# Second MoE matmul of an attention + MoE kernel: seven block products per granule pair in place of eight

## The chip, the cores and the metric

The kernel runs on one core of a Trainium2 chip. The metric is the device time in microseconds (us) of one execution. Executions of the kernel before agree within 0.4%. A run more than 1.5% above the fastest of the same kernel is labelled slow and left out of the ratios. The profile is of one execution; its span (first to last instruction) is about 2 us shorter than the measured time. Each experiment ran in the same rounds and on the same chip as the kernel before, whose medians lie between 217.01 and 217.14 us in the five batches; two experiments are compared with each other only through it.

Engines: TensorE (PE in the profile, its weight loads PEld), VectorE (DVE), ScalarE (ACT), GpSimd (POOL); SP is the queue that issues most DMAs (79 of 155 in the trace before, 74 from GpSimd's).

## The reference

```python
# q, k, v: [4, 8, 768, 64]; 8 global keys, 96 local keys
scores = q @ k.T / 8 + bias(distance, head)        # masked outside global or local keys
x = (softmax(scores) @ v) -> [3072, 512]           # heads side by side
h = x @ w_in                                       # [3072, 2048]
g = s * relu(h) ** 2 + b
out = g @ w_out                                    # [3072, 512], float32
```

The two last lines are computed as `s * (relu(h)**2 @ w_out) + b * colsum(w_out)`, so the second MoE matmul takes the squares in bf16, and its evacuation from PSUM multiplies by `s` and adds the constant row `bvec`.

## The kernel before: the parts that matter

The 3072 tokens are cut into 12 granules of 256 tokens. Attention of granule j takes two *steps*, 2j and 2j+1, each of two head pairs. The MoE work of earlier granules is put between the pieces of attention, so that TensorE always has something to do. In the traces VectorE and TensorE run their instructions in the order of the program (VectorE's timeline below, 107.57 to 115.01 us, and PE's, 143.85 to 155.97 us, are two such stretches).

```python
def p1_mm(j, fp):                 # two 128-row blocks of h for granule j
    ps = ps_h.tile([P, 2, GT], F32, tag="psh")            # 3 PSUM buffers "psh" in all
    for i in range(2):
        for kc in range(KC):      # 4: 8 matmuls of 256 columns in all
            nc.tensor.matmul(ps[:, i, :], lhsT=w_in_bf[...], rhs=xT[j][:, kc, :], ...)
    def relu():   nc.scalar.activation(gs, ps[:], ACT.Relu)             # ScalarE
    def square(): nc.vector.tensor_tensor(gs, gs, gs, ALU.mult)         # VectorE, 512 wide

def p2_mm(j, tb):                 # second matmul: 128 tokens, 16 matmuls of 512 columns
    po = ps_h.tile([P, DM], F32, tag="psh")
    for fc in range(FC):
        nc.tensor.matmul(po[:], lhsT=gT[j][:, fc, tb*P:(tb+1)*P], rhs=w_out_bf[:, fc, :], ...)

def p2_out(j, tb):                # VectorE evacuates: s * po + bvec, then DMA out
    nc.vector.scalar_tensor_tensor(out=o_sb[:], in0=po, scalar=s_bc[:], in1=bvec[:],
                                   op0=ALU.mult, op1=ALU.add)

def stage_A(u):                   # attention-value product of one head pair
    av = ps_av.tile(...)          # the ONLY attention buffer in PSUM
    ... matmuls pt x (v or voff) ...
    normalize(xn, av)             # VectorE: reciprocal and product; only then is av free

def step(s, c0, c1, c2):
    run(scores(s + 1))            # scores, exp (ScalarE), mask (VectorE) of the next step
    if first step of the granule: make_voff(j)            # VectorE copies the shifted values
    run(c0);  stage_A(2 * s);     flush()                 # flush: output evacuations
    if first step: make_koff(j + 1)
    run(c1);  stage_A(2 * s + 1); run(c2)
    if last step of the granule: finish_granule(j)        # DMA-transposes xn[j] into xT[j]

# the steady schedule: in each step one p2 (128 tokens) and four p1 pieces (...)
for j in range(7, NJ):
    step(2*j,     p2[j-3][1:2], p1[j-2][4:6], p1[j-2][6:8])
    step(2*j + 1, p2[j-2][0:1], p1[j-1][0:2], p1[j-1][2:4])
```

The softmax here doesn't subtract the row's maximum and nothing guards it: scores larger than these inputs give would overflow.

## Time and profile before

| | before |
|---|---|
| median time | 217.11 us (216.98 to 217.18, 4 runs) |
| span of the profile | 215.4 us |
| PE busy, idle (span less busy) | 209.8, 5.6 us |
| DVE busy | 140.5 us |
| mean granted TensorE clock | 0.999 |

The page's first part gives busy time by engine, the second the busy tenths of each fortieth of the span; PEclk is the granted TensorE clock in tenths (9 is 90% or more).

```profile
PE 209.8 (97%) x2013; PEld 143.8 (67%) x2013; DVE 140.5 (65%) x344; ACT 113.6 (53%) x175; POOL 67.0 (31%) x89
...
PE   6999999999999999999999999999999999999993
...
PEclk9999999999999999999999999999999999999999
```

TensorE is busy in every slice. From the chain of waits (start in us, length, engine, tile and line, number of instructions), one step:

```profile
136.73 0.44 PE ps_s L395 x12
137.18 3.56 PE ps L611 x16
140.74 0.18 PE ps_av L446 x6
140.92 1.75 PE ps L566 x16
142.66 0.18 PE ps_av L446 x6
142.84 1.75 PE ps L566 x16
```

Each piece starts where the last one ends, so TensorE alone sets the pace: a step is 3.5 us of second matmul (16 of 512 columns, 216 ns from start to start), twice 1.75 us of first matmul (16 of 256 columns, 109 ns each) and the small attention products. The waits view of PE, which lists what it waited for, holds one line for everything after 85 us (the columns: total us, times, longest):

```profile
PE ps_av L446 <- DVE xn L420: 0.2, 1, 0.2
```

The groups that give the costs (busy, mean ns of one, then idle before them and its releaser):

```profile
L579 DVE TENSOR_TENSOR gT<-gT 128x512 bf16<-128x512 bf16 x96 | 40.4, 424 | 24.2 <-ACT gT L576 22.2
...
L411 DVE TENSOR_TENSOR pt<-pt,tmpl 128x1024 bf16<-128x1024 bf16 (+1 forms) x40 | 25.6, 650 | 9.3 <-ACT pt L404 8.6
...
L622 DVE SCALAR_TENSOR_TENSOR o_sb<-ps,s_bc,bvec 128x512 f32<-128x512 f32 x19 | 14.1, 744 | 9.9 <-PE ps L611 9.9
```

A bf16 product on VectorE costs 0.424 us for 512 elements and, in the 1024-wide form of the second line alone, 0.693 us; an evacuation of 512 costs 0.744 us. VectorE is idle for a third of the time, and that idle time is what the change means to use.

### The profile page before, as it was taken

The numbers are of one execution on the slowest core, as the hardware profiler recorded it, in microseconds if no ns is written. First come the engines' busy times: TensorE is split into PE (matmuls) and PEld (weight loads), VectorE is DVE, ScalarE is ACT, GpSimd is POOL, SyncE is SP. The second block draws the span as 40 slices with busy tenths as digits, with TensorE's granted clock in tenths as the row PEclk, the third lists the DMA queues.
The fourth block names the chain that finished last, engine by engine and source line by source line (L and its number), as shares of the span: only waits on it lengthen the run. The fifth ranks groups of instructions, "written<-read, shape, count | busy, mean of one in ns | idle before, by whom it ended". The sixth has DMA issues, their size and how long they took to land.

```text
span 215.4 us, 4939 instructions
## 1 busy us (share of the span) xinstructions
PE 209.8 (97%) x2013; PEld 143.8 (67%) x2013; DVE 140.5 (65%) x344; ACT 113.6 (53%) x175; POOL 67.0 (31%) x89
## 2 busy tenths in 40 slices
PE   6999999999999999999999999999999999999993
PEld 2578885557866575776676676676676676665852
DVE  3497579995989668985675675666676663432421
ACT  4675668585975564554644643544644642240610
POOL 8873335897646104506318045000000000000000
PEclk9999999999999999999999999999999999999999
DMA  5999999999999997999999949952310310311102
GB/s 166 197 177 206 207 206 173 152 152 127 117 150 138 157 183 110 156 255 171 208 133 171 171 79 159 132 102 72 97 50 5 97 52 24 73 52 49 49 3 97
DMA packets 107079, 27.33 MB, mean 127 GB/s; under 512 B 97712, under 2 KB 104112, under 8 KB 107056
## 3 DMA queue, kind: packets, MB, share of 16 engines
q0 software_dynamic: 72864, 12.85, 82.2%
q1 hardware_dynamic: 33136, 13.64, 34.5%
q10 hardware_dynamic: 1056, 0.52, 0.9%
q8 instruction: 16, 0.26, 0.5%
q14 instruction: 7, 0.06, 0.1%
HBM read 27.26 MB, written 6.29 MB: 156 GB/s over the span
## 4 chain that ended last, share of the span: by engine, by line
PE 91%; DVE 5%; DMA 2%; issue 0%
PE ps L566 38%; PE ps L611 35%; PE ps_s L395 5%; PE ps_av L446 5%; DMA first<-in_k_dram 2%; PE ps_2c L668 2%; DVE pt L411 1%; PE ps_t L269 1%; PE ps_s L372 1%; PE ps_w L155 1%; PE ps_s L468 1%; PE ps_x L542 1%; PE ps_t L301 1%; DVE o_early L644 1%; DVE wsum L589 1%; DVE xn L420 1%
## 5 line engine op out<-in xcount | busy, mean ns | idle before, releaser
L576 ACT ACTIVATE gT<-ps 128x512 bf16<-128x512 f32 x96 | 57.0, 598 | 76.4 <-PE ps L566 76.4
L566 PE MATMUL ps<-xT,w_in_bf 128*128 128x256 bf16 x768 | 90.2, 273 | 0.0
L611 PE MATMUL ps<-w_out_bf,gT 128*128 128x512 bf16 x368 | 83.9, 380 | 0.0
L566 PEld LDWEIGHTS <-w_in_bf 128*128 128x128 bf16 x768 | 72.7, 98 | 8.9
L611 PEld LDWEIGHTS <-gT 128*128 128x128 bf16 x368 | 34.4, 98 | 39.2
L579 DVE TENSOR_TENSOR gT<-gT 128x512 bf16<-128x512 bf16 x96 | 40.4, 424 | 24.2 <-ACT gT L576 22.2
L404 ACT ACTIVATE pt<-ps_s 128x1024 bf16<-128x1024 f32 (+1 forms) x44 | 39.2, 948 | 6.4 <-PE ps_s L395 6.4
L411 DVE TENSOR_TENSOR pt<-pt,tmpl 128x1024 bf16<-128x1024 bf16 (+1 forms) x40 | 25.6, 650 | 9.3 <-ACT pt L404 8.6
L104 POOL DMA_DIRECT2D nat<-in_k_dram x22 | 19.7, 895 | 8.1 <-DMA w_in_bf<-in_moe_w_in_dram 3.0
L104 POOL DMA_DIRECT2D nat<-in_q_dram x22 | 19.6, 891 | 8.3 <-DMA w_out_bf<-in_moe_w_out_dram 3.4
L105 POOL DMA_DIRECT2D vb<-in_v_dram x22 | 19.8, 900 | 5.7 <-DMA w_out_bf<-in_moe_w_out_dram 2.1
L420 DVE TENSOR_TENSOR xn<-ps_av,rc 128x256 bf16<-128x256 f32 x48 | 20.4, 425 | 1.7
L622 DVE SCALAR_TENSOR_TENSOR o_sb<-ps,s_bc,bvec 128x512 f32<-128x512 f32 x19 | 14.1, 744 | 9.9 <-PE ps L611 9.9
L446 PEld LDWEIGHTS <-pt 128*128 128x128 bf16 x320 | 14.6, 97 | 5.9 <-DVE xn L420 0.8
L419 DVE RECIPROCAL rc<-ps_av 128x4 f32<-128x4 f32 x48 | 8.5, 178 | 14.8 <-PE ps_av L446 13.5
L446 PE MATMUL ps_av<-vb,pt 128*128 128x65 bf16 x208 | 15.4, 193 | 0.4 <-DVE xn L420 0.2
L110 POOL COPY gate<-xT 1x1 bf16<-1x1 bf16 x6 | 1.2, 202 | 40.6 <-DMA xT<-xn 37.9
L446 PE MATMUL ps_av<-voff,pt 128*128 128x65 bf16 x112 | 10.5, 193 | 0.0
L395 PE MATMUL ps_s<-qk 64*128 64x128 bf16 x208 | 10.0, 224 | 0.0
L589 DVE TENSOR_TENSOR wsum<-wsum,w_out_bf 128x512 f32<-128x512 f32 x14 | 9.6, 686 | 0.2
L395 PEld LDWEIGHTS <-qk 64*128 64x128 bf16 x208 | 6.2, 96 | 5.3 <-issue 3.2
L155 PE MATMUL ps_w<-idle 128*128 128x256 bf16 (+1 forms) x19 | 5.2, 434 | 1.2 <-DVE idle L145 1.2
(77 smaller groups left out, 107.6 us busy)
## 6 DMA issues: line engine op xcount, KB each, us to landing
out_dram<-o_sb SPq DMA_DIRECT2D x19, 256.0 KB, 3.5
nat<-in_k_dram POOLq DMA_DIRECT2D x22, 128.0 KB, 7.5
nat<-in_q_dram POOLq DMA_DIRECT2D x22, 128.0 KB, 7.4
vb<-in_v_dram POOLq DMA_DIRECT2D x22, 128.0 KB, 7.5
w_in_bf<-in_moe_w_in_dram POOLq DMA_DIRECT2D x4, 512.0 KB, 11.6
w_out_bf<-in_moe_w_out_dram POOLq DMA_DIRECT2D x4, 512.0 KB, 17.9
out_dram<-o_early SPq DMA_DIRECT2D x4, 256.0 KB, 6.6
first<-in_q_dram ACTq DMA_DIRECT2D x2, 256.0 KB, 4.9
```

What stands on the lines that cost most here:

```text
L104: nc.gpsimd.dma_start(t[:, n, i, :, :], rows_of(srcs[n], b, sb))
L105: nc.gpsimd.dma_start(vbuf[b % 2][:, sb, :, 0:D], rows_of(v, b, sb))
L395: nc.tensor.matmul(ps[:, hi, oc * P : (oc + 1) * P], lhsT=kt[rows], rhs=qt[rows], start=not bias, stop=not bias or part * GB + n == len(pl ...
L404: nc.scalar.activation(pt[:, :, 0:ncol], ps[:, :, 0:ncol], ACT.Exp, scale=QSCALE)
L411: nc.vector.tensor_tensor(pv, pv, m.rearrange("p h a c -> p h (a c)"), ALU.mult)
L420: nc.vector.tensor_tensor(dst, av[:, :, :, 0:D], rc[:].to_broadcast((P, 2, 2, D)), ALU.mult)
L446: nc.tensor.matmul(av[:, i, hi, 0 : D + 1], lhsT=pt[:, hi, c * P : (c + 1) * P], rhs=vv, start=(n == 0), stop=(n == len(terms) - 1),)
L566: nc.tensor.matmul(ps[:, i, :], lhsT=w_in_bf[:, kc, fc * P : (fc + 1) * P], rhs=xT[j][:, kc, :], start=(kc == 0), stop=(kc == KC - 1),)
L576: nc.scalar.activation(gs, ps[:], ACT.Relu)
L579: nc.vector.tensor_tensor(gs, gs, gs, ALU.mult)
L611: nc.tensor.matmul(po[:], lhsT=gT[j][:, fc, tb * P : (tb + 1) * P], rhs=w_out_bf[:, fc, :], start=(fc == 0), stop=(fc == FC - 1),)
L622: nc.vector.scalar_tensor_tensor(out=o_sb[:], in0=po_cur.pop((j, tb))[:], scalar=s_bc[:], in1=bvec[:], op0=ALU.mult, op1=ALU.add,)
```

## The change

For granules 4 to 11 two granules A and B (256 tokens each) and the two halves of the 2048 inner rows make a 2 x 2 block matrix; so do the halves of the inner rows and of the 512 output columns of `w_out`. The Strassen-Winograd form needs seven block products instead of eight, with sums of blocks before and after. TensorE's second matmul falls by an eighth; VectorE gets the sums.

```diff
+    weight_sums: t1 = w12 - w11;  t2 = w22 - t1;  t3 = w22 - w12 (into w12);  t4 = w21 - t2     # 2048 wide, once
+    def g_sums(j, q):                      # j is the odd granule; q a quarter of its first matmul; 1024 wide
+        if q < 2:  s3 = A1 - B1
+        else:      s1 = B1 + B2;  s2 = s1 - A1;  s4 = A2 - s2
+    def unit_p1(j, q):                     # four blocks of h at a time
+        for fp in (2*q, 2*q + 1): p1_mm; relu
+        nc.vector.tensor_tensor(gs, gs, gs, ALU.mult)          # one square, 1024 wide
+        if j % 2: g_sums(j, q)
+    def product(pr, n):                    # 2 x 8 matmuls of 256 columns into one "psh" buffer
+        1: A1 w11   2: A2 w21   3: s4 w22   4: B2 t4   5: s1 t1   6: s2 t2   7: s3 t3
+    def evac(pr, n):                       # VectorE, from PSUM
+        1: r = s*P1 + bias (twice)   6: r += s*P6 (both, 1024 wide)   5: r1 += s*P5
+        2: store r0 + s*P2           7: store r1 + s*P7; r0 += s*P7
+        3: store r1 + s*P3           4: store r0 + s*P4
@@ step @@
         stage_A(2 * s + 1, pool)
+        flush()
@@ schedule (u1(j, q) is unit_p1, pe(pair, n) a product and its evacuation) @@
-    step(13, p2[4][0:1], p1[5][0:2], p1[5][2:4])
-    for j in range(7, NJ):
-        step(2 * j, p2[j - 3][1:2], p1[j - 2][4:6], p1[j - 2][6:8])
-        step(2 * j + 1, p2[j - 2][0:1], p1[j - 1][0:2], p1[j - 1][2:4])
+    step(12, [rest(3, 1)], [u1(4, 2)], [u1(4, 3)] + weight_sums[1:2])
+    step(13, [u1(5, 0), u1(5, 1)], [u1(5, 2)], [u1(5, 3)] + weight_sums[2:4] + spread)
+    step(14, [pe(2, 1), pe(2, 2)], [pe(2, 6), pe(2, 5)], [u1(6, 0)])
+    for j in (7, 9, 11):                   # pr = (j - 3) // 2
+        if j > 7: step(2 * j, [pe(pr, 2), pe(pr, 6)], [pe(pr, 5)], [u1(j - 1, 0)])
+        step(2 * j + 1, [pe(pr, 7), pe(pr, 3)], [pe(pr, 4)], [u1(j - 1, 1)])
+        step(2 * j + 2, [u1(j - 1, 2), u1(j - 1, 3)], [pe(pr + 1, 1)], [u1(j, 0)])
+        step(2 * j + 3, [u1(j, 1), u1(j, 2)], [u1(j, 3)], [])            # "odd step": all late sums
```

(Abbreviated; tiles that were needed only early share memory with the new ones. The last pair runs after the attention, with products in the order 1, 2, 7, 5, 6, 4, 3.)

## The prediction

> **What bounds the kernel now.** TensorE. The page gives PE 97% busy of a 215.4 us span, DVE 65%, ACT 53%. The waits view for PE from 105 us to the end is empty, and the chain of waits is 91% PE, running from 89 us on as an unbroken series of matmul groups. A two-head-pair step lasts 8.08 us, of which second matmul 3.45, first matmul 3.5, scores 0.55, attention-value about 0.5.
>
> **What the change removes.** In the chain a 256-column matmul costs 109 ns (32 in 3.49 us) and a 512-column one 216 ns (16 in 3.45 us)[...]. So splitting columns is nearly free and seven for eight is real: per granule pair 64 x 216 = 13.8 us becomes 112 x 109 = 12.2 us. Four pairs: about 6.7 us off PE, all critical. That is the whole possible gain (3.1%).
>
> **What it adds, on VectorE.** Durations read: bf16 product 512 wide 0.424, 1024 wide 0.693, output evacuation 512 wide 0.743; instructions without a dependency follow about 0.08 closer than these. 2048 wide then is about 1.2 (estimate from the slope), the PSUM evacuation 1024 wide 1.2-1.3 (estimate). [...] Per pair: eight sums +5.2; evacuations 7.0 in place of 3.0; wide squares -1.6. Once: four weight sums +4.9. Total +35 us: DVE about 175 us busy.
>
> **How much is on the critical path.** From the granule-4 stage to the end of attention (about 88-184 us) a pair's four steps hold about 30.6 us of PE work and 29 us of DVE work even at the closer spacing. The average nearly fits; its distribution doesn't. The step finishing an odd granule has 6.35 us of PE work but about 9.1 us of DVE work (two masks, squares, all sums). Its second attention-value product needs the only attention PSUM buffer, whose normalize stands in the in-order DVE queue behind the sums. Walking the steps by hand with the durations above:
> - that step: PE waits about 2.3 us for normalize; twice.
> - the following steps: about 1.4 us per pair for PSUM buffers whose evacuations come late, and for the transposed attention output, whose source is normalized late (landing now 3.2 us); twice.
> - first pair: the last two weight sums follow the sums at the end of step 13; the fourth product (5) then waits about 4 us for the evacuation of product 1; other waits 2.5 us.
> - tail: the last evacuations queue on DVE, about 1.2 us.
> Sum about +14 to 15 us of PE waits against -6.7; some may overlap better than I walked, so I take +13.
>
> **Prediction: 223.5 us, 217 to 228 in 8 of 10.** Faster by over 2%: 0.09; within 2%: 0.28; slower by over 2%: 0.63.
>
> **Right if** PE busy falls below about 93%, matmul count rises by about 190, second-product matmuls stay near 109 ns each in unbroken runs; DVE busy is near 175 us; the chain of waits shows much more DVE (normalize, sums, evacuations); PE or its weight loads idle before attention-value matmuls on normalize, before products and first matmuls on PSUM evacuations; one gap of several us in the first products.
>
> **Wrong if** 1024-wide sums on strided halves are much cheaper or dearer than 0.69; DVE spacing is closer so that lag never reaches the single attention buffer (then about 211-214); PE really runs slower for these products (weight loads 98 ns against 109 leave little slack), or its clock drops after the long gap (then above 228).

The two estimates of VectorE follow from the trace before. The product grows by 0.269 us from 512 to 1024 wide (0.424 to 0.693), so 2048 wide comes to 1.23; the changed kernel's weight sums took 1.21 to 1.22. Evacuations of 128, 384 and 512 took 0.352, 0.618 and 0.744 us (L676 and L622), so 1024 comes to 1.28; those of the changed kernel took 1.275 to 1.285 (L775). The closer spacing of 0.08 us is there too: the copy after the 0.74 us evacuation from 141.51 starts at 142.17.

## The result and the profile after

The changed kernel took 231.80 us (231.25 to 234.41, 4 runs) against 217.11. Ratios here are the mean time of one kernel's fast runs over the mean of the other's in the same rounds, so they are not quite the ratios of the medians: 1.07 (95% interval 1.0645 to 1.0756), so 7% slower. The prediction said 223.5, within 217 to 228: the direction was right, the size was not.

The page of the changed kernel:

```profile
PE 210.0 (92%) x2189; PEld 163.6 (71%) x2189; DVE 175.8 (77%) x364; ACT 114.2 (50%) x178; POOL 68.8 (30%) x89
...
PE   6999999999999999998298999699999699999981
...
PEclk9999999999999999999979999979999979999998
```

TensorE's busy time is the same as before although it does an eighth less of the second matmul in granules 4 to 11, PE now shows slices of 2 and 6 inside, and PEclk dips to 7 in three slices. Spans and clocks:

| | before | after | difference |
|---|---|---|---|
| span | 215.4 | 229.5 | +14.1 |
| PE idle (span less PE busy) | 5.6 | 19.5 | +13.9 |
| PE busy | 209.8 | 210.0 | +0.2 |
| DVE busy | 140.5 | 175.8 | +35.3 |
| mean granted clock | 0.999 | 0.973 | |

Run 8 below, with the same arithmetic and the full clock up to its last matmul, has 204.3 us of PE busy time. So the +0.2 is two things: about -5.5 us of matmul work saved and about +5.7 us of slower matmuls. (The clock record, read alone, gives 5.1 us for the latter: three stretches of 3.41 us at half clock. A fourth begins after the last matmul; it lowers the mean clock and costs nothing.)

PE's waits from the same point on:

```profile
PE ps_av L447 <- DVE xn L421: 5.3, 4, 2.2
PE ps_av L447 <- DVE voff L354: 4.3, 1, 4.3
PE ps_last L766 <- DVE o_last L775: 1.9, 1, 1.9
```

Part of the same waits is listed with the weight loads, which now come first in a wait. The chain of waits in an odd step (step 17), where before it was TensorE alone:

```profile
143.81 0.61 ACT gT L581
...
144.44 0.70 DVE gT L741
...
145.16 0.70 DVE gsum L731
...
145.89 0.70 DVE gsum L732
...
146.61 0.69 DVE gsum L733
...
147.43 0.44 DVE xn L421
...
148.77 5.27 PE ps L766 x32
```

ScalarE's relu releases the square (gT), then come three sums (gsum), and only then the normalize (xn) that frees the one attention buffer for TensorE. The last line holds the second effect, slow matmuls: 32 of 256 columns took 5.27 us where 32 take 3.5. The timeline of PE shows the same place (last bracket: idle before, and releaser):

```profile
143.85 1.91 PE L571 MATMUL ps<-xT,w_in_bf 128*128 128x256 bf16 x16
147.91 0.20 PE L447 MATMUL ps_av<-vb,pt 128*128 128x65 bf16 x1 [2.15 <-DVE xn L421]
...
148.70 3.56 PE L766 MATMUL ps<-w_out_bf,gT 128*128 128x256 bf16 x16
152.05 1.99 PE L766 MATMUL ps<-wsub,gsum 128*128 128x256 bf16 x16
...
154.06 1.91 PE L766 MATMUL ps<-wsub,gsum 128*128 128x256 bf16 x16
```

After 2.15 us of idle the 16 matmuls from 148.70 reach 152.05, 3.35 us, and the next 16 need 1.8 us as usual: for some 3 us TensorE ran at about half speed (209 ns a matmul in place of 109). The windows view (stretch and its length, PE busy and matmuls, granted clock, then DMA) has the stretch with the wait and the one after it:

```profile
145.37:148.78 3.41, 1.26 (x25) 1.00 1.14 48
148.78:152.19 3.41, 3.41 (x17) 0.50 0.00 0
```

The longest wait is in the first pair, and its cause stands in VectorE's timeline (columns as before):

```profile
114.87 0.21 PE L447 MATMUL ps_av<-voff,pt 128*128 128x65 bf16 x1 [4.26 <-DVE voff L354]
```

```profile
107.57 0.68 DVE L741 TENSOR_TENSOR gT<-gT 128x1024 bf16<-128x1024 bf16 x1
108.29 0.69 DVE L731 TENSOR_TENSOR gsum<-gT 128x1024 bf16<-128x1024 bf16 x1
109.01 0.69 DVE L732 TENSOR_TENSOR gsum<-gsum,gT 128x1024 bf16<-128x1024 bf16 x1
109.74 0.69 DVE L733 TENSOR_TENSOR gsum<-gT,gsum 128x1024 bf16<-128x1024 bf16 x1
110.35 1.22 DVE L707 TENSOR_TENSOR w_out_bf<-w_out_bf 128x2048 bf16<-128x2048 bf16 x1
111.48 1.21 DVE L708 TENSOR_TENSOR wsub<-w_out_bf,wsub 128x2048 bf16<-128x2048 bf16 x1
112.62 1.28 DVE L412 TENSOR_TENSOR pt<-pt,tmpl 128x1024 bf16<-128x1024 bf16 x2
113.83 0.42 DVE L350 COPY voff<-vb 128x1056 bf16<-128x1056 bf16 x1
114.28 0.73 DVE L354 COPY voff<-vb 8x528 bf16<-8x528 bf16 x2
```

TensorE finished products 1 and 2 at about 110.6 and then needed the shifted values (voff). VectorE was working without a pause on a square, three sums, two weight sums and two masks that stood ahead of that copy. TensorE waited 4.26 us.

### The profile page after: what moved, and what is told of

It is laid out like the page before. It is cut to its first block, busy times and chain, and to the rows that moved or that the text cites. A ratio compares the mean times of both kernels' runs of the same rounds, so it can differ in the third digit from the quotient of the medians.

```text
span 229.5 us, 5323 instructions
## 1 busy us (share of the span) xinstructions
PE 210.0 (92%) x2189; PEld 163.6 (71%) x2189; DVE 175.8 (77%) x364; ACT 114.2 (50%) x178; POOL 68.8 (30%) x89
## 4 chain that ended last, share of the span: by engine, by line
PE 74%; DVE 17%; DMA 3%; ACT 3%; issue 2%; DVEq 0%; ACTq 0%; SPq 0%
PE ps L571 32%; PE ps L766 18%; PE ps L619 10%; PE ps_av L447 4%; PE ps_s L396 4%; DVE xn L421 2%; DVE gT L741 2%; DMA first<-in_k_dram 2%; DVE pt L412 1%; DVE base L775 1%; ACT pt L405 1%; ACT gT L581 1%; DVE gsum L732 1%; DVE gsum L731 1%; DVE gsum L733 1%
## 5 line engine op out<-in xcount | busy, mean ns | idle before, releaser
L741 DVE TENSOR_TENSOR gT<-gT 128x1024 bf16<-128x1024 bf16 x32 | 22.1, 689 | 11.1 <-ACT gT L581 11.0
L766 PEld LDWEIGHTS <-gsum 128*128 128x128 bf16 x256 | 25.5, 101 | 5.9 <-issue 2.1
L619 PE MATMUL ps<-w_out_bf,gT 128*128 128x512 bf16 x128 | 29.7, 380 | 0.0
L412 DVE TENSOR_TENSOR pt<-pt,tmpl 128x1024 bf16<-128x1024 bf16 (+1 forms) x40 | 24.9, 646 | 4.2 <-ACT pt L405 4.1
L766 PEld LDWEIGHTS <-gT 128*128 128x128 bf16 x192 | 19.4, 104 | 3.6 <-issue 0.2
L619 PEld LDWEIGHTS <-gT 128*128 128x128 bf16 x128 | 11.7, 97 | 13.1
L420 DVE RECIPROCAL rc<-ps_av 128x4 f32<-128x4 f32 x48 | 8.5, 177 | 13.9 <-PE ps_av L447 12.4
L766 PE MATMUL ps<-w_out_bf,gT 128*128 128x256 bf16 x128 | 17.8, 301 | 0.0
L584 DVE TENSOR_TENSOR gT<-gT 128x512 bf16<-128x512 bf16 x32 | 13.2, 422 | 5.4 <-ACT gT L581 5.0
L110 POOL COPY gate<-xT 1x1 bf16<-1x1 bf16 x6 | 2.5, 421 | 49.4 <-DMA xT<-xn 46.7
L766 PE MATMUL ps<-wsub,gsum 128*128 128x256 bf16 x128 | 16.4, 288 | 0.0
```

The costliest lines, as they stand in the source:

```text
L412: nc.vector.tensor_tensor(pv, pv, m.rearrange("p h a c -> p h (a c)"), ALU.mult)
L619: nc.tensor.matmul(po[:], lhsT=g_of(j)[:, fc, tb * P : (tb + 1) * P], rhs=w_out_bf[:, fc, :], start=(fc == 0), stop=(fc == FC - 1),)
L766: nc.tensor.matmul(ps[:, tb, :], lhsT=stat[:, fc, tb * P : (tb + 1) * P], rhs=mov[:, fc, :], start=(fc == 0), stop=(fc == NH - 1),)
```

## The experiments

Two theories were set against each other from the start. **Queue position**: what hurts is where the sums stand in VectorE's in-order queue, ahead of something TensorE waits for. **Throughput**: VectorE simply got too much work, and any order costs the same. A third suspect was TensorE itself (narrower matmuls, more weight loads). To these the trace added the **clock**: slow matmuls after a wait.

### 1. No quarter sums

```diff
-        if j % 2:
-            g_sums(j, q)
-    stationary of products 3, 5, 6, 7: the sums
+    stationary of products 3, 5, 6, 7: plain quarters      # wrong result on purpose
```

> The 32 quarter sums are left out and the four sum products read plain quarters (wrong result on purpose); products, evacuations and weight sums stay. Queue-position theory (the sums stand in the in-order VectorE queue ahead of a normalize, a value copy and evacuations, and the TensorE clock drops after each such wait): the two waits of about 2.2 us in the odd steps go, so does most of the 4.3 us wait of the first pair, and with them about 4.5 us of slow matmuls: about 218 us (216 to 220), clock above 0.985. Throughput rival (VectorE simply has too much work; 22.5 of the 35 us added are taken out, so the same share of the loss comes back): about 222 us. TensorE rival (seven 256-wide products with more weight loads are slower than they look): about 230 us.

Measured: 219.76 us, ratio 1.0116 (1.0094 to 1.0138), clock 0.996. The sums account for about 12 of the 14.7 us. That is more than their share of the added work (throughput said 222) and inside the range that queue position gave, near its upper end (216 to 220).

### 2. No weight sums

```diff
-    t1 = w12 - w11;  t2 = w22 - t1;  t3 = w22 - w12;  t4 = w21 - t2
+    t1, t2, t3, t4 = w11, w22, w12, w21                     # wrong result on purpose
```

> The four weight sums are left out (plain weight blocks in their place, wrong result on purpose). Queue-position theory: only the first pair gains; its 4.3 us wait shrinks by at least the 2.4 us of the two sums that stand before the value copy, and the slow matmuls after it (1.4 us) go: 227.5 us (226.5 to 229). Throughput rival: 4.9 of 35 us added, so about 2 us: 229.7. TensorE rival: no change.

Measured: 227.58 us, ratio 1.0485 (1.0462 to 1.0509), clock 0.988. Four instructions of together 4.9 us cost about 4 us, as queue position expected (227.5).

### 3. The tail

```diff
-    ps = ps_sc.tile(...)                    # one tile for both halves of the last product
     for tb in range(GB):
+        ps = ps_sc.tile(...)                # one each
         product(pr, 3, [tb], ...)
-        o = work.tile(..., tag="o_sb", bufs=3)
+        o = work.tile(..., tag="first", bufs=4)
```

> Only the last product: its two halves get their own PSUM tiles, and its output tiles their own buffers. If the tail lost time to the shared tile (1.9 us wait of TensorE) and to the wait for the output buffer (1.35 us), the end comes 1.5 to 2.7 us earlier: about 229.5 us. If the end is set by the queue of evacuations alone: under 0.7 us gained.

Measured: 230.82 us, ratio 1.0628 (1.0596 to 1.0660). About 1 us less than the changed kernel, not as much as expected and not clear of noise: the two intervals overlap (1.0645 to 1.0756 for the changed kernel). The 1.9 us wait of the last product is gone from the trace, but the evacuations queue up on VectorE all the same.

### 4. Only the products

No quarter sums, no weight sums, mended tail (edits of 1 to 3 together).

> No quarter sums, no weight sums, and the mended tail (wrong result on purpose): the seven products with their evacuations alone. Queue-position theory: TensorE never waits long, keeps its clock (above 0.99) and shows the whole saving of 6.7 us less about 1 to 2 us of tail: 211 to 213 us. TensorE rival (more, narrower matmuls cost more than 109 ns): 218 us or more. If the clock drops come from the denser weight loads and not from waits, the clock stays at 0.97 here too.

Measured: 219.02 us, ratio 1.006 (1.003 to 1.009; one slow run left out), clock 0.993. A miss: expected 211 to 213. The products were not slow, though: 32 of 256 columns took 3.5 us wherever nothing waited. Where the saving went, the waits view of PE shows:

```profile
PE ps L571 <- DMA xT<-xn: 2.8, 1, 2.8
PE ps_av L447 <- DVE voff L354: 0.8, 1, 0.8
```

The new schedule asks for the first matmul of granule 5 at the start of step 13, half a step earlier than before, and its input comes by DMA transpose; that transfer took 7.3 us in this trace, so TensorE waited 2.8 us. (In the kernel before these transfers took 3.2 us in the median, but up to 7.3 too, with no wait: the earlier request is what is new.) Part of the rest is the tail: PE's last matmul ends 5.1 us before the end of the span, before it was about 3.3. So even without any sums the new schedule gave back what the seven products had saved.

### 5. Dummy matmuls in the waits

```diff
+    def keep_busy(n):    # n matmuls of 512 columns into a spare score buffer
-    step(14, [pe(2, 1), pe(2, 2)], ...
+    step(14, [pe(2, 1), pe(2, 2), keep_busy(18)], ...
-        step(2 * j + 3, [u1(j, 1), u1(j, 2)], [u1(j, 3)], [])
+        step(2 * j + 3, [u1(j, 1), u1(j, 2)], [u1(j, 3), keep_busy(9)], [])
```

> The changed kernel with dummy matmuls into a spare score buffer in the three longest TensorE waits: 18 of 512 columns (about 3.9 us) before the attention-value product of the first pair's product step, 9 (about 1.9 us) in each of the two later odd steps. They fit in the waits, so the waits for VectorE end when they did. If the clock drops because TensorE idles, the granted clock rises from 0.973 to above 0.99 and the slow matmuls (about 1.4 + 2.3 + 1.5 us against their usual pace) go: about 227 us (226 to 228.5). If the drops have another cause [...], the clock stays near 0.97 and the time at 231 to 233.

Measured: 228.88 us, ratio 1.0533 (1.0511 to 1.0554), clock 0.995. The clock came back, as the clock theory said. In the profiled execution the clock is below full only from 224.9 us on, after TensorE's last matmul (223.4). The time gained is 2.9 us, not 4.8: span less PE busy is 13.9 us, and the dummies themselves take 8.2, so TensorE did no useful work for 22.1 us against 19.5. The dummies did not hold up the useful work: after each of the three groups TensorE still waited for VectorE (0.71, 0.21 and 0.21 us). I read this as TensorE arriving earlier, with fast matmuls, and waiting longer; a new wait of 0.60 us for a value copy (at 186.7) fits, but no run shows it separately.

### 6. Order alone, first pair

```diff
-    step(13, ..., [u1(5, 3)] + weight_sums[2:4] + spread)
-    step(14, ..., [u1(6, 0)])
+    step(13, ..., [u1(5, 3)] + spread)
+    step(14, ..., [u1(6, 0)] + weight_sums[2:4])
```

> Order only: the last two weight sums stand at the end of the next step in VectorE's queue, behind the value copy and the first evacuations; every instruction stays. Queue-position theory: as good as leaving out all four, since only their place hurt: 228 us (227 to 229). Throughput rival: same work, same time: 231 to 232.

Measured: 230.99 us, ratio 1.0651 (1.0599 to 1.0702); the interval overlaps that of the changed kernel. A miss for queue position. The wait for the value copy fell from 4.3 to 1.7 us, but the moved sum became a wait of its own (the DMA line is the same kind as in experiment 4):

```profile
PE ps L571 <- DMA xT<-xn: 4.0, 2, 2.7
PE ps L766 <- DVE w_out_bf L707: 2.0, 1, 2.0
...
PE ps_av L447 <- DVE voff L354: 1.7, 1, 1.7
```

### 7. Order alone, second and third pair

```diff
     odd step:   normalize first, then s1, s2;   s3 and s4 one step later
-    step(2 * j + 2, [u1(j - 1, 2), u1(j - 1, 3)], [pe(pr + 1, 1)], [u1(j, 0)])
-    step(2 * j + 3, [u1(j, 1), u1(j, 2)], [u1(j, 3)], [])
+    step(2 * j + 2, [u1(j - 1, 2), u1(j - 1, 3)], [], [u1(j, 0)])
+    step(2 * j + 3, [u1(j, 1), u1(j, 2)], [u1(j, 3)], [pe(pr + 1, 1)])
```

> Order and place only, in the second and third pairs, the same instructions: normalize before quarter sums, the sums that product 6 needs first, the others a step later, product 1 moved from the even step to the odd one (which had three blocks of TensorE work against four), product 4 before 3. Queue-position theory: the waits of about 2.2 us on normalize go below 0.7, with them the clock drops after them; some waits of 0.3 to 1 us appear instead: 225 us (223.5 to 227.5). Throughput rival: VectorE busy time is unchanged, so the time is too: 230 to 232.

Measured: 230.26 us, ratio 1.0622 (1.0585 to 1.0658). Another miss. The wait in the odd step did go, but in the even step nothing was left between the two attention-value products, and the second now waits there 1.7 us for the normalize of the first (1.73 and 1.72 us, at 138.7 and 172.0).

### 8. All of it together

The order of 7 for all three pairs; products 1 and 2 of the first pair pulled ahead, so that its sums spread over three steps; the mended tail. The arithmetic is that of the changed kernel.

```diff
-    step(13, [u1(5, 0), u1(5, 1)], [u1(5, 2)], [u1(5, 3)] + weight_sums[2:4] + spread)
-    step(14, [pe(2, 1), pe(2, 2)], [pe(2, 6), pe(2, 5)], [u1(6, 0)])
-    step(15, [pe(2, 7), pe(2, 3)], [pe(2, 4)], [u1(6, 1)])
+    step(13, [pe(2, 1), u1(5, 0)], [u1(5, 1)], [u1(5, 2)] + weight_sums[2:4])
+    step(14, [u1(5, 3), pe(2, 2)], [u1(6, 0)], [pe(2, 6)])
+    step(15, [pe(2, 5), pe(2, 7)], [pe(2, 4)], [pe(2, 3), u1(6, 1)])
```

> All of it in one: the order of the last run for all three pairs, the first pair's products 1 and 2 pulled ahead so that its sums spread over three steps, weight sums where VectorE has room, first matmuls of granule 5 a block later than in the changed kernel, the mended tail. Same arithmetic as the changed kernel. Queue-position theory: no wait over 1.5 us, clock above 0.99, 217 us (214.5 to 220), so at best a little under the kernel before. Throughput rival: above 225.

Measured: 223.46 us, ratio 1.029 (1.0271 to 1.0308; one slow run left out), clock 0.995 in the profiled run. The same arithmetic, placed differently, is 8 us faster than the changed kernel, so throughput alone is not the cause. But PE is still idle for 17.1 us of the span (19.5 in the changed kernel). By the account of the span, most of the 8 us is the clock: PE busy fell from 210.0 to 204.3 us, idle time by 2.4. The waits had become shorter and more numerous; their sum had not fallen much.

### 9. One block back between the attention products

```diff
-        step(2 * j + 2, [u1(j - 1, 2), u1(j - 1, 3)], [], [u1(j, 0)])
+        step(2 * j + 2, [u1(j - 1, 2)], [u1(j - 1, 3)], [u1(j, 0)])
```

> The combined order with one correction: in the even steps one first-matmul unit stands again between the two attention-value products; the combined order had put both before, so that the second product followed the first at once and waited about 2.2 us for the normalize of the only attention buffer. Same instructions, same engines. Queue-position theory (what stands between a release and its waiter decides): both 2.2 us waits go: 219 us (217.5 to 220.5). Throughput rival: VectorE work is the same, so no change: 223 to 224.

Measured: 223.48 us, ratio 1.031 (1.0277 to 1.0342). No gain at all, the clearest miss. The waits view of PE, first of run 8, then of run 9:

```profile
PE ps_av L447 <- DVE xn L421: 3.7, 3, 1.7
...
PE ps_av L447 <- DVE voff L354: 1.9, 2, 1.4
```

```profile
PE ps_av L447 <- DVE voff L354: 4.9, 4, 1.5
...
PE ps_av L447 <- DVE xn L421: 0.2, 1, 0.2
```

The expectation took the two waits for about 2.2 us each; in run 8's trace they are 1.72. The wait for the normalize (3.7 us) turned into a wait for the value copy (1.9 to 4.9 us). Only one block of TensorE work now stood ahead of the first attention-value product, and the copy it needs stands behind the masks, which stand behind the exp of the next step. A step has one block fewer than it needs to cover both.

### 10. Work moved to other engines

```diff
-            tt(s3, A1, B1, ALU.subtract)                            # VectorE
+            (nc.gpsimd if j > 5 else nc.vector).tensor_tensor(s3, A1, B1, ALU.subtract)
-            make_voff(j)
+            make_voff(j, copy=acp if j % 2 else cp)                 # ScalarE in odd granules
     the last pair: two evacuations ahead of product 6's
```

> As the last, with VectorE work moved away: the value copies of the odd granules on ScalarE, the difference of the first quarters of the last three pairs (6 instructions) on GpSimd, and the last pair's evacuations reordered so that two of them run before product 6 ends. Queue-position and throughput theories both expect gains; by the waits on the value copy (about 1.9 us in the combined run) and about 0.5 us of tail: 216.8 us (215 to 219), level with the kernel before. If GpSimd's writes get in VectorE's way, VectorE's own instructions become longer and nothing is gained.

Measured: 226.19 us, ratio 1.0442 (1.0412 to 1.0472), slower than without. The case named last in the expectation came true. GpSimd needed 2.38 us for a sum that took VectorE 0.69, and VectorE's own instructions grew. VectorE groups between 88 and 190 us of this run (the masks and the first sum; 688 and 691 ns in the changed kernel):

```profile
L412 DVE TENSOR_TENSOR pt<-pt,tmpl 128x1024 bf16<-128x1024 bf16 x16 | 12.4, 805 | 1.0 <-ACT pt L405 0.9
...
L742 DVE TENSOR_TENSOR gsum<-gT 128x1024 bf16<-128x1024 bf16 x6 | 6.8, 1140 | 0.0
```

The means hide where: of the eight first sums in the whole run, the three that ran beside a GpSimd sum took 2.06, 2.06 and 2.50 us, the other five 0.68 to 0.69, and the masks that did took up to 2.59. So in this run it was beside a GpSimd sum that these instructions of VectorE grew; that GpSimd's writes are the reason, as the expectation has it, was not shown.

### 11. Seven products for the last pair only

```diff
     granules 4 to 9: steps, second matmul and evacuation as in the kernel before
     granules 10, 11, after the attention: the seven products, tail as in 10
     weight sums t1, t2 in steps 18 and 20, t3, t4 after the attention
```

> Seven products only for the last granule pair, after the attention, where VectorE was mostly idle; all other granules as in the kernel before, with its steps. The weight sums in steps with room. If the saving holds wherever VectorE has room: 1.7 us of TensorE work less, about 1.3 us of longer end: 216.7 us (215.7 to 217.5), so within noise of the kernel before or a little under it; no clock drop, clock above 0.997. If the seven products cost time by themselves: above 218.

Measured: 215.77 us against 217.05, ratio 0.9944 (0.9931 to 0.9956), clock 0.999, result correct. This is the one version that beats the kernel before, by 0.6% (less than the 2% that would count as faster, but clear of noise), and it ran a little better than expected. It holds the reordered tail too, and no run separates the two. Of the waits of PE after 85 us, the largest is 0.3 us:

```profile
PE ps_av L447 <- DVE xn L421: 0.3, 1, 0.3
```

### 12 and 13. A made wait in the kernel before

To see the clock alone: the kernel before, with no part of the change, gets seven useless VectorE products ahead of a normalize in two steps. The second kernel also fills the wait.

```diff
         run(c0)
+        if s in (17, 21): hold_vector(7)      # 7 VectorE products, 1024 wide, into scratch
         stage_A(2 * s)
         ...
         run(c1)
+        if s in (17, 21): keep_busy(10)       # second kernel only
         stage_A(2 * s + 1, pool)
```

> The kernel before, with no part of the change, and seven useless VectorE products of 1024 elements ahead of the first normalize in two steps (17 and 21), so that the second attention-value product of each waits about 2.5 us, as in the changed kernel. If idle time of TensorE by itself lowers the clock: about 2 x 2.5 us of waiting and 2 x 1 to 1.8 us of slow matmuls after, clock 0.98 to 0.99, 224.5 us (223 to 226). If a wait costs only itself: clock 0.998, 222 us (221 to 222.8).

> The same, with ten dummy matmuls of 512 columns (2.2 us) in each made wait. If idle time lowers the clock, the clock stays at 0.998 here and the time is the wait alone: about 222 us (221 to 223), 2 to 3 us less than its partner. If not, the two are equal.

Measured: empty 222.96 us (222.11 to 225.55), ratio 1.029 (1.0244 to 1.0337); filled 222.25 us (222.07 to 222.55), ratio 1.0241 (1.0228 to 1.0254). In the profiled execution of the empty one PE waited as planned:

```profile
PE ps_av L446 <- DVE xn L420: 5.1, 3, 2.7
```

The executions, with their granted clocks:

```
empty:   222.11 (1.000)  222.18 (1.000)  222.27 (1.000)  223.66 (0.992)  225.42 (0.982)   [225.55 (0.985), labelled slow]
filled:  222.07 (1.000)  222.10 (0.997)  222.39 (1.000)  222.55 (0.998)
```

Both predictions for the empty one are half right. Two waits (2.21 and 2.65 us in the trace) always cost themselves, 5 us. In some executions they also cost the clock, and then up to 3.3 us more; in three of the five fast ones they did not. With the wait filled, the clock stayed in all four. So with the idle time of TensorE left empty the clock was 0.992 and 0.982 in two fast executions and 1.000 in three, and with it filled 0.997 to 1.000.

The traces show what goes with it. In each of them, all stretches at half clock begin on one grid with steps of 3.41 us (in the changed kernel at 114.65, 148.78, 182.91 and 227.29 us, so 10, 10 and 13 steps apart). Over the 15 traces, after the first 20 us, every step in which PE was idle for 1.97 us or more is followed by a step at half clock (28 of 28), and no step with 1.92 us or less is (0 of 854). Run 6 holds both nearest cases, in the windows view (the step after the third, 226.78 to 230.19, has clock 1.00):

```profile
182.41:185.82 3.41, 1.44 (x29) 1.00 0.00 0
185.82:189.23 3.41, 3.41 (x18) 0.50 0.07 14
...
223.37:226.78 3.41, 1.49 (x14) 1.00 0.23 76
```

In the changed kernel the steps from 111.23, 145.37 and 179.50 us hold 3.41, 2.15 and 2.15 us of idle time: each gap of 2.15 us lay within one step. After 20 us the only other step of its trace with 2 us or more is the tail's (2.38 us from 223.87, followed by the stretch from 227.29); the next longest is 1.20 us (from 220.46), and after it the clock stayed at 1.00. In the profiled execution of the empty kernel the two gaps (2.21 and 2.65 us) fall across an edge of the grid, no step has more than 1.47 us, and the clock stayed. So in these traces what separates the gaps that were followed by half clock from those that were not is where they fell on the grid. (Worked out from these traces alone; the two fast executions of the empty kernel that lost clock left no trace.)

## Why the prediction was right or wrong

**What bounds the kernel: right.** The chain of waits before was TensorE alone, and in the changed kernel it is not.

**The saving: right in kind, a little small.** Predicted 6.7 us; 209.8 less 204.3 (run 8) is 5.5 us, less 203.8 (run 9) 6.0, but eight matmul records are missing from run 9's trace. The prediction's 109 and 216 ns held; where the remaining 0.7 to 1.2 us went was not traced.

**VectorE's added work: right.** "DVE about 175 us busy": measured 175.8. The sums took 0.69 us each, as read from the masks.

**The waits: the mechanism right, the sum right partly by luck and too small underneath.** "I take +13": PE idle grew by 13.9 us. The 2.3 us wait for normalize in each odd step was 2.15 us in the trace. The first pair's gap of "about 4 us" was 4.26, though for the value copy in the same queue and not, as walked, for an evacuation. Three terms were mis-sized, and they partly offset each other. "The following steps: about 1.4 us per pair", twice, did not appear: PE was busy for 16.5 of the 16.6 us from 123.0 to 139.6 and for 16.0 of the 16.1 from 157.9 to 174.0. The tail was put at 1.2 us: from the end of the last block of first matmuls (213.1) to the end of the span are 16.4 us, where six products of 1.75 us and the 3.3 us that the kernel before needs after its last matmul make 13.8, so 2.6. And the first matmul of granule 5, pulled ahead of its DMA transpose, was not named in the sum, unless it is among the first pair's "other waits 2.5 us": in the changed kernel TensorE waits 1.0 us there (the list of PE puts it down to ScalarE, that of the weight loads, with 1.1 us, to the DMA transpose), in experiment 4 2.8 us for the DMA.

**The failed step: "Sum about +14 to 15 us of PE waits against -6.7".** The sum has only waits in it. The clock stood under "wrong if", outside the sum and only for "the long gap" ("then above 228"); that branch came true. In the trace it is 5 to 6 us of slower matmuls (5.1 by the clock record, 5.7 by PE busy time), and they follow gaps of 2.15 us too. -5.5 saved, +13.9 idle and +5.7 slow give the 14.1 us of the span. The two effects are not independent: run 5 shows that giving the clock back returns 2.9 us, because TensorE then waits about 2.6 us longer for VectorE. So of the 8.3 us missed, the experiment puts 2.9 on the clock; most of the rest is waiting that the prediction undercounted and that the slow matmuls partly hid (22.1 us without useful work in run 5 against 5.6 before, so 16.5 where the prediction took 13).

The stretches of 3.41 us lie on a grid that stands differently in each trace: from the start of the span its first edge is at 2.0 us in the changed kernel, 3.3 in the kernel before and 1.5 in run 6. A step need not be idle throughout for half clock to follow: 1.97 us of idle time in one step were enough (run 6), so gaps shorter than the step were. The prediction had tied the drop to the long gap alone.

**Queue position or throughput?** Neither as stated. Leaving the sums out gives 12 us, and placing them differently gives 8 us with the same arithmetic (about 1 us of it may be the mended tail), so order matters. But runs 6, 7 and 9 each removed one wait and got another of nearly the same length. Over a pair's four steps I estimate from the durations above 29 us of VectorE work for 30.6 us of TensorE work (in the trace of the changed kernel VectorE is busy for 27.1 and 29.6 us in the two pairs' stretches of 34.9 and 35.1 us), and each step needs several things from VectorE early (masks, value copy, normalize, evacuations). At that load a wait that was removed came back elsewhere. What reordering did buy in run 8 was mostly shorter waits, which kept the clock. That no order of this work would reach 217 us was not shown; the four that were tried (runs 6 to 9) did not.

## What to carry to other kernels

Work saved on the bounding engine is worth its time only where the engine that pays for it has room *in that stage and ahead of that stage's deadlines*; here the seven products lost 7% when four pairs used them, three of these inside the attention, and gained 0.6% when only the last pair did, after it. When walking a schedule by hand, add to a TensorE wait of some 2 us or more the chance of slow matmuls after it (each of the waits of 4.26, 2.15 and 2.15 us was followed by a 3.41 us step at clock 0.50, which costs up to 1.7 us; after the made waits of 2.21 and 2.65 us the clock stayed in three of five fast executions), and follow every consumer of the in-order queue, not only the obvious one. When a reordering removes a wait, look in the trace for where it went before believing in the next one.
